# Moving the loads and splits of the first two head pairs around the bias stage of an attention kernel

## The chip, the cores and the metric

The kernel runs on one core of a Trainium2 chip. The metric is the device time of one execution in microseconds. Three runs of the kernel before took 463.45, 464.14 and 468.85; the median, 464.14, is what the change is compared with. All other times here are microseconds from the start of the span of one profiled execution.

## The reference

Attention with a learned relative-position bias, then two mixture-of-experts stages. The change touches the first part alone:

```python
scores = scale * np.matmul(q, k.transpose(0, 1, 3, 2))
rel = (pos[:, None] - pos[None, :]).astype(np.float32)
psi_rel = np.log1p(np.abs(rel))
psi_i = np.log1p(np.maximum(pos[:, None].astype(np.float32), 1.0))
x = (psi_rel / psi_i)[..., None]
h = np.maximum(x @ w1 + b1, 0.0)          # 32 hidden units
bias = h @ w2                             # 8 heads
scores = scores + bias.transpose(2, 0, 1)[None, :, :, :]
...                                       # softmax over the last axis
return np.matmul(attn, v).astype(np.float32)
```

q, k and v are 4 x 8 x 576 x 64 (batch, heads, sequence, head size). The bias is the same for all four batches; w1, b1 and w2 are inputs, so it has to be computed.

## The kernel before

**Constants.** Small tables and the weights of the bias network come first, some in SyncE's queue (`sel`, `pib`, `ident`, `phi_sb`, `w10`, part of `wsm`), some in ScalarE's (`ll`, the log table of 576 KB; the rest of `wsm`; `ipi`). A first matmul of `sel` and `wsm` spreads the weights over the partitions. VectorE copies them (`wrp`, `w2b`), scales the tables `pib`, `nib` and `ll` by them, and rounds `ident` to `identr`.

**Bias stage.** 36 batches `bt`, in the order 16..23, 0..15, 32..35, 24..31. One batch makes four hidden tiles `hid` of 128 x 576 (L215 on VectorE, L217 on ScalarE for one tile of three batches in four; 12 buffers), multiplies them with `w2b` on TensorE (L219), evicts the result on ScalarE to `ev` (L222; 6 buffers), and stores `ev` through SyncE to `scratch` in DRAM (L224). After batches 23, 7, 15, 35 and 31 SyncE loads the finished bias rows of the first head pair back from `scratch` (L285; L288 to L290 for the short last tile `biasm`). SyncE issues in program order, so what stands behind such a load waits with it.

**Attention.** 16 units, called pairs here: a pair of heads of one batch. For each, `tq`, `tk` and `tn` are loaded (`LQ`, `LK`, `LV`; one buffer each for `tq` and `tk`), and GpSimd splits q and k into a rounded high part (L383: `QHI`, `KHI`) and a low part (L385: `QLO`, `KLO`) in `sq` and `sk`, one buffer each. TensorE transposes these (L416, L444), ScalarE evicts them to `k` and `qT`, and the score matmuls follow (L461). VectorE adds the bias (L478), ScalarE takes the exponential (L485), GpSimd makes a high fp16 part of it (L496, `HI`), VectorE the low part (L500, `LO`), and SyncE transposes both by DMA. GpSimd also makes the low part of v (L404, `VLO`) and a swapped copy of k (L433, `SW`).

**What sets the order.** A table `SCHED` gives each step of a pair a due time. The steps before the first score matmul, and for the second pair `LK`, `LQ`, `KHI`, `KLO`, `QHI`, `QLO` (the function `x_early`), are written out before the bias stage (`early`); all others follow it in the order of their due times. In the bias stage only SyncE's queue is fixed to the written order. The other engines are ordered there by a scheduler from a model of the timeline; behind the bias stage all engines keep the written order.

Of the kernel before, what the change touches and what calls it, by code (L numbers as in the profile page):

```python
# [9 lines left out]
F32 = mybir.dt.float32  # L10
# [4 lines left out]
ALU = mybir.AluOpType  # L15
# [5 lines left out]
P = 128  # L21
NU = 9
HID = 32
# [89 lines left out]
def soft_moe_attention_kernel(ctx, tc, q, k, v, w1, b1, w2, phi, mw1, mw2,  # L113
                              skip, gate, gw1, gw2, c_ll, c_pi, c_ipi, c_sel, c_id, c_rk, out):
    nc = tc.nc
    sync, act, vec, pool, pe = nc.sync, nc.scalar, nc.vector, nc.gpsimd, nc.tensor
# [5 lines left out]
    ident = const.tile([P, P], F32, name="ident")  # L122
    sel = const.tile([P, P], F32, name="sel")
    phi_sb = const.tile([P, 4, NSL], F32, name="phi_sb")
# [3 lines left out]
    identr = const.tile([P, P], F32R, name="identr")  # L128
# [8 lines left out]
    w10 = const.tile([P, 4, 10], F32, name="w10")  # L137
# [19 lines left out]
    ps_t = actx.enter_context(tc.tile_pool(name="ps_t", bufs=2, space=PSUM))  # L157
# [5 lines left out]
    with ExitStack():  # L163
# [3 lines left out]
        ll = bc.tile([P, LLW], F32, name="ll")  # L167
        pib = bc.tile([P, 144], F32, name="pib")
        nib = bc.tile([P, 144], F32, name="nib")
        ipi = bc.tile([P, 36], F32, name="ipi")  # L170
        wsm = bc.tile([HID, 10], F32, name="wsm")
        wrp = bc.tile([P, 10], F32, name="wrp")
        w2b = bc.tile([P, 32], F32, name="w2b")
        offs = [bc.tile([P, 1], F32, name=f"offs{i}") for i in range(2)]
        vec.memset(w2b, 0.0)
        vec.memset(offs[0], 0.0)
        sync.dma_start(out=sel, in_=c_sel)
        act.dma_start(out=wsm[:, 0:1], in_=w1.rearrange("o m -> m o"))
        sync.dma_start(out=wsm[:, 2:10], in_=w2)
        act.dma_start(out=wsm[:, 1:2], in_=b1.rearrange("(m o) -> m o", o=1))  # L180
        sync.dma_start(out=pib, in_=c_pi)
        act.dma_start(out=ll, in_=c_ll)
        act.dma_start(out=ipi, in_=c_ipi)
        sync.dma_start(out=ident, in_=c_id)
        sync.dma_start(out=phi_sb, in_=phi.rearrange("(k p) s -> p k s", p=P))
        sync.dma_start(out=w10[:, :, 0:8], in_=gate.rearrange("(k p) e -> p k e", p=P))
        sync.dma_start(out=w10[:, :, 8:9], in_=skip.rearrange("(k p o) -> p k o", p=P, o=1))
        pw = ps_t.tile([P, 512], F32, name="pt")
        pe.matmul(pw[:, 0:10], lhsT=sel[0:HID, :], rhs=wsm, start=True, stop=True)
        vec.tensor_copy(wrp, pw[:, 0:10])  # L190
        for g in range(4):
            vec.tensor_copy(w2b[g * 32:(g + 1) * 32, g * 8:(g + 1) * 8], wrp[g * 32:(g + 1) * 32, 2:10])
        vec.tensor_scalar(out=pib, in0=pib, scalar1=wrp[:, 1:2], scalar2=None, op0=ALU.mult)
        vec.tensor_scalar(out=nib, in0=pib, scalar1=-1.0, scalar2=None, op0=ALU.mult)
        vec.tensor_scalar(out=ll, in0=ll, scalar1=wrp[:, 0:1], scalar2=None, op0=ALU.mult)
        vec.tensor_copy(identr, ident)

        po = ps_t.tile([P, 512], F32, name="pt")
        for c in range(4):
            pe.matmul(po[c * 32:(c + 1) * 32, 0:1], lhsT=w2b, rhs=wrp[:, 1:2], start=True, stop=True)  # L200
        vec.tensor_scalar(out=offs[1], in0=po[:, 0:1], scalar1=-1.0, scalar2=None, op0=ALU.mult)
        vec.tensor_copy(offs[0][0:96], offs[1][0:96])

        def bias_batch(bt):
            r, m4 = bt // 4, bt % 4
# [583 lines left out]
    OPS = [ops_of(n) for n in range(NP)]  # L789
# [6 lines left out]
    def x_early(x):  # L796
        return x in ("LK", "LQ", "KHI", "KLO", "QHI", "QLO")

    todo = sorted((n * II + place(n, x), n, x) for n in range(NP) for x in OPS[n])
    first = min(SC[x] for x in SC if x[:2] == "QK")  # L800
    early = [y for y in todo if y[0] < first or y[1] == 1 and x_early(y[2])]
    for t_, n, x in early:
        if (n, x) != (0, "SW"):
            OPS[n][x]()
    todo = [y for y in todo if y not in early]

# [2 lines left out]
    with tc.manual_schedule(engines={mybir.EngineType.SP}):  # L809
        for bt in order:  # L810
            bias_batch(bt)
            if bt % 8 == 7 or bt == 35:
                load_bias(0, bt // 8)
            if bt == 3:
                OPS[0]["SW"]()
    bctx.close()
    wctx = ExitStack()
    xpool = ctx.enter_context(tc.tile_pool(name="xpool", bufs=1, side="right"))
# [6 lines left out]
    with tc.manual_schedule(engines=fixed):  # L825
        last_td = max(place(NP - 1, f"TD{t}") for t in range(3)) + (NP - 1) * II
        lead_after = last_bias[0].ins
        lead = next(y for y in todo if y[2][0] == "L" and y[2][1] in "KQV" or y[2][:2] == "TD")
        for y in todo:
            t_, n, x = y  # L830
            with tc.issue_after(lead_after) if y == lead else ExitStack():
                OPS[n][x]()
            if t_ == last_td:
                while len(wq) < NW + 10:
                    weight_piece()
# [24 lines left out]
    SW = const.tile([P, 10], F32R, name="SW")  # L860
# [17 lines left out]
    held, sis = [], sl[1]  # L878
# [9 lines left out]
    with ExitStack() as mctx:  # L888
# [38 lines left out]
        for i in range(32):  # L927
            e, r = i // 4, i % 4
            o = e * P + r * NSL
            for j in range(4):  # L930
                pe.matmul(ph[j * 32:(j + 1) * 32, :], lhsT=sT[:, o:o + NSL],
                          rhs=wq[i][:, j * 256:(j + 1) * 256], start=(i == 0), stop=(i == 31))
# [6 lines left out]
        pt = ps.tile([P, 512], F32, name="pc")  # L939
# [550 lines left out]
```

## Time and profile before

| what | value |
|---|---|
| median of three runs | 464.14 |
| profiled execution | 465.27 |
| its span | 463.4 |
| busy: TensorE, VectorE, ScalarE, GpSimd | 416.3, 356.1, 309.5, 277.4 |
| mean granted TensorE clock | 0.985 |
| HBM read, written | 63.82 MB, 15.34 MB |

The span is what lies between the first and the last instruction; the execution takes 1.9 more. The busy sums cover stages with different limits. The bias stage takes up the first 64 us or so, the 16 pairs about the next 250, and the rest is weight loading and the two expert stages. For this change the views by time are of use: the timeline of one engine over the first 90 us, what ended each of its idle times, and when transfers landed.

### The profile page before, as it was taken

How to read it: one execution, taken by the hardware profiler on the slowest of the kernel's cores; microseconds unless marked ns; L12 is line 12 of the kernel's file. 1: busy time of each engine (PE TensorE's matmuls, PEld its weight loads, DVE VectorE, ACT ScalarE, POOL GpSimd, SP SyncE). 2: the span in 40 equal slices, each digit the busy share in tenths (PEclk: the TensorE clock that was granted, in tenths of full speed). 3: DMA queues.
4: the chain of work that ended last, by engine and by line, in shares of the span. 5: the costliest groups of instructions: out<-in, count | busy, mean ns of one | idle time of the engine just before them, and what ended most of it. 6: DMA issues, size and time to landing. Idle time of an engine off the chain costs nothing.

```text
span 463.4 us, 11519 instructions
## 1 busy us (share of the span) xinstructions
PE 416.3 (90%) x4314; PEld 303.8 (66%) x4314; DVE 356.1 (77%) x824; ACT 309.5 (67%) x650; POOL 277.4 (60%) x241
## 2 busy tenths in 40 slices
PE   3989997999999999999999999988899688899993
PEld 2545466887988888888888888786545221246572
DVE  5999977989889988988999978989645800118883
ACT  3997869798998998898889888697321300028710
POOL 4599508999999999999999989856120000001100
PEclk9999998999999999999999999999999889999998
DMA  6578768799988988998999997969999999992076
GB/s 179 197 240 269 269 231 212 199 168 217 247 204 170 247 197 171 228 233 185 190 230 241 167 218 135 191 127 198 302 412 407 404 410 409 409 343 102 24 204 214
DMA packets 145883, 108.92 MB, mean 235 GB/s; under 512 B 117952, under 2 KB 120512, under 8 KB 145824
## 3 DMA queue, kind: packets, MB, share of 16 engines
q1 hardware_dynamic: 143920, 104.91, 83.3%
q10 hardware_dynamic: 1824, 2.97, 2.0%
q8 instruction: 36, 0.59, 0.5%
q0 software_dynamic: 80, 0.26, 0.2%
q14 instruction: 23, 0.19, 0.1%
HBM read 63.82 MB, written 15.34 MB: 171 GB/s over the span
## 4 chain that ended last, share of the span: by engine, by line
PE 35%; DMA 21%; DVE 20%; POOL 8%; issue 7%; ACT 6%; ACTq 0%; SPq 0%; DVEq 0%; POOLq 0%
DVE ehl L500 9%; PE sc L461 7%; DMA x<-in_moe_w_dram 7%; DMA k<-in_moe_w_dram 6%; DVE e L478 5%; PE sc L219 5%; ACT ev L222 2%; PE pt L553 2%; DMA w2e<-in_moe_w_dram 2%; DMA tn<-in_v_dram 2%; PE av L590 2%; DMA bias<-in_moe_w_dram 2%; POOL k L433 1%; PE pt L696 1%; DVE em L478 1%
## 5 line engine op out<-in xcount | busy, mean ns | idle before, releaser
L485 ACT ACTIVATE e<-e,st 128x576 f32<-128x576 f32 x128 | 97.6, 776 | 16.1 <-DVE st L478 15.2
L478 DVE CUSTOM_DVE_ANT_0 e<-sc,bias 128x576 f32<-128x576 f32 x128 | 94.6, 749 | 13.0 <-PE sc L461 12.2
L461 PE MATMUL sc<-k,qT 128*128 128x288 f32 x512 | 96.9, 317 | 8.3 <-DVE st L478 6.0
L500 DVE SCALAR_TENSOR_TENSOR ehl<-e,ehl 128x1152 f16<-128x1152 f32 x48 | 88.7, 1867 | 0.9 <-POOL ehl L496 0.7
L461 PEld LDWEIGHTS sc<-k,qT 128*128 128x128 f32 x512 | 72.8, 191 | 18.8 <-DVE st L478 6.7
L496 POOL TENSOR_SCALAR ehl<-e 128x1152 f16<-128x1152 f32 x48 | 57.9, 1214 | 10.6 <-ACT e L485 8.9
L433 POOL TENSOR_SCALAR k<-k 64x1152 fp32r<-64x1152 f32 x30 | 59.8, 1995 | 3.0 <-ACT k L449 0.7
L219 PE MATMUL sc<-hid,w2b 128*32 128x288 f32 x576 | 52.7, 426 | 6.4 <-DVE hid L215 3.2
L215 DVE TENSOR_SCALAR hid<-ll,nib 128x576 f32<-128x576 f32 x117 | 56.7, 568 | 0.0
L590 PE MATMUL av<-v,eT 128*128 128x65 f16 x1152 | 50.0, 194 | 0.0
L219 PEld LDWEIGHTS sc<-hid,w2b 128*32 128x32 f32 x576 | 27.2, 112 | 29.7 <-ACT ev L222 12.9
L590 PEld LDWEIGHTS <-eT 128*128 128x128 f16 x1152 | 44.1, 98 | 0.6
L383 POOL TENSOR_SCALAR sk<-tk 128x576 fp32r<-128x576 f32 x16 | 39.7, 2484 | 5.4 <-PE pt L444 5.3
L1161 POOL TENSOR_SCALAR Lt<-rk 128x128 f16<-128x128 f32 x1 | 0.3, 297 | 66.6 <-PE pbig L1047 66.6
L222 ACT ACTIVATE ev<-sc,offs,ipi 128x576 f32<-128x576 f32 x36 | 30.0, 834 | 8.8 <-PE sc L219 6.8
L404 POOL TENSOR_TENSOR v<-tv,v 128x650 f16<-128x650 f32 x16 | 22.9, 1432 | 17.8 <-ACT v L400 17.8
L598 PE MATMUL av<-eq,tv 128*64 128x192 f32 x320 | 29.5, 331 | 0.0
L553 PE MATMUL pt<-ident,e 128*128 128x128 f32 x144 | 24.5, 282 | 4.5 <-DVE xnat L660 2.4
L1008 DVE COPY part<-pbig 128x256 f32<-128x256 f32 x2 | 0.9, 426 | 34.5 <-ACT part L1007 34.5
L1007 ACT COPY part<-pbig 128x256 f32<-128x256 f32 x2 | 0.7, 372 | 37.5 <-PE pbig L1047 37.5
L385 POOL TENSOR_TENSOR sq<-tq,sq 128x576 fp32r<-128x576 f32 x16 | 24.2, 1515 | 0.3
L598 PEld LDWEIGHTS av<-eq,tv 128*64 128x64 f32 x320 | 21.6, 137 | 4.2 <-issue 1.0
(338 smaller groups left out, 890.6 us busy)
## 6 DMA issues: line engine op xcount, KB each, us to landing
scratch<-ev SPq DMA_DIRECT2D x36, 288.0 KB, 4.7
bias<-scratch SPq DMA_DIRECT2D x16, 576.0 KB, 4.7
x<-in_moe_w_dram SPq DMA_DIRECT2D x18, 512.0 KB, 10.2
k<-in_moe_w_dram SPq DMA_DIRECT2D x14, 512.0 KB, 10.2
bias<-in_moe_w_dram SPq DMA_DIRECT2D x13, 512.0 KB, 9.3
tq<-in_q_dram SPq DMA_DIRECT2D x16, 288.0 KB, 3.8
tk<-in_k_dram SPq DMA_DIRECT2D x16, 288.0 KB, 4.7
tn<-in_v_dram SPq DMA_DIRECT2D x16, 288.0 KB, 4.9
```

Source lines behind the costliest of these rows:

```text
L215: vec.tensor_scalar(out=hid, in0=src, scalar1=nib[:, gi:gi + 1], scalar2=None, op0=ALU.max)
L219: pe.matmul(pb[c * 32:(c + 1) * 32, hh, 0:288], lhsT=w2b, rhs=hid[:, hh * 288:(hh + 1) * 288], start=True, stop=True)
L222: act.activation(ev, pb[:, :, 0:288].rearrange("p a (l u) -> p u a l", u=NU), AF.Identity, bias=offs[not on_act], scale=ipi[:, bt:bt + 1])
L383: pool.tensor_scalar(out=sx[:, :, 0, :], in0=t, scalar1=1.0, scalar2=1.0, op0=ALU.mult, op1=ALU.mult)
L433: pool.tensor_scalar(out=k1[64 * i:64 * i + 64], in0=k0[64 - 64 * i:128 - 64 * i], scalar1=1.0, scalar2=1.0, op0=ALU.mult, op1=ALU.mult)
L461: pe.matmul(sc[:, hh, 0:288], lhsT=l_, rhs=kf[i][:, o:o + 288], start=(i == 0), stop=(i == 1))
L478: vec.tensor_tensor_reduce(out=z["e", t][:, o].rearrange("p (a j) -> p a j", a=2), in0=z.pop(("sc", t, j))[:, :, 0:288], in1=bias_t[hp, t] ...
L485: act.activation(ee, ee, AF.Exp, bias=z["m", t][:, j:j + 1], scale=-1.0, **kw)
L496: pool.tensor_scalar(out=eh[:, 0], in0=z["e", t], scalar1=ES, scalar2=1.0, op0=ALU.mult, op1=ALU.mult)
L500: vec.scalar_tensor_tensor(out=eh[:, 1], in0=z.pop(("e", t)), scalar=ES, in1=eh[:, 0], op0=ALU.mult, op1=ALU.subtract)
L590: pe.matmul(av[:, oj:oj + VD], lhsT=eT[:, ei, 5 * j + c], rhs=v16[:, vi, 6 * j + c], start=False, stop=lastt and k_ == 2 and c == 3)
L598: pe.matmul(z["av", 1][j * 64:(j + 1) * 64, o], lhsT=tv[:, 6 * j + c if c < 4 else 4 + j, 0:64], rhs=z["eq"][:, 4 * j + c if c < 4 else 8] ...
```

## The change

The constants, their loads and the first matmuls become a function `prepare()`, which is called after the steps of all pairs have been defined. In it `LQ` of the first pair is the first load in SyncE's queue and `LK` the fifth; the log table is the first in ScalarE's. The six early steps of the second pair leave the place ahead of the bias stage: `LK` and `LQ` are written behind the store of batch 26, the third of the last eight, and `KHI`, `KLO`, `QHI`, `QLO` behind the whole stage, ahead of all its other steps. No instruction is added or taken away.

```diff
-        act.dma_start(out=wsm[:, 0:1], in_=w1.rearrange("o m -> m o"))
...
-        act.dma_start(out=ll, in_=c_ll)
...
+        def prepare():
+            vec.memset(w2b, 0.0)
+            vec.memset(offs[0], 0.0)
+            OPS[0]["LQ"]()
+            act.dma_start(out=ll, in_=c_ll)
+            sync.dma_start(out=sel, in_=c_sel)
+            act.dma_start(out=wsm[:, 0:1], in_=w1.rearrange("o m -> m o"))
+            act.dma_start(out=wsm[:, 1:2], in_=b1.rearrange("(m o) -> m o", o=1))
+            sync.dma_start(out=wsm[:, 2:10], in_=w2)
+            act.dma_start(out=ipi, in_=c_ipi)
+            sync.dma_start(out=pib, in_=c_pi)
+            OPS[0]["LK"]()
+            sync.dma_start(out=ident, in_=c_id)
...
     early = [y for y in todo if y[0] < first or y[1] == 1 and x_early(y[2])]
+    prepare()
+    held = [y for y in early if y[1] == 1 and x_early(y[2])]
     for t_, n, x in early:
-        if (n, x) != (0, "SW"):
+        if (n, x) not in ((0, "SW"), (0, "LQ"), (0, "LK")) and (t_, n, x) not in held:
             OPS[n][x]()
...
             if bt == 3:
                 OPS[0]["SW"]()
+            if bt == 26:
+                OPS[1]["LK"]()
+                OPS[1]["LQ"]()
...
         lead_after = last_bias[0].ins
+        for x in ("KHI", "KLO", "QHI", "QLO"):
+            OPS[1][x]()
```

SyncE's queue at the start of the program, before (the second `tq` is that of the second pair; its `tk` follows behind the store that stands last here; line numbers are those of each kernel):

```order
L177 DMA sel<-in_c_sel_dram 128x128
L179 DMA wsm<-in_w_dram 32x8
L181 DMA pib<-in_c_pi_dram 128x144
L184 DMA ident<-in_c_id_dram 128x128
L185 DMA phi_sb<-in_moe_phi_dram 128x4x32
L186 DMA w_73<-in_moe_w_gate_dram 128x4x8
L187 DMA w_73<-in_moe_w_skip_dram 128x4x1
L354 DMA tq<-in_q_dram 128x576
L349 DMA tk<-in_k_dram 128x576
L359 DMA tn<-in_v_dram 128x576 x2
L354 DMA tq<-in_q_dram 128x576
L224 DMA scratch<-ev 128x576
```

and now:

```order
L357 DMA tq<-in_q_dram 128x576
L180 DMA sel<-in_c_sel_dram 128x128
L183 DMA wsm<-in_w_dram 32x8
L185 DMA pib<-in_c_pi_dram 128x144
L352 DMA tk<-in_k_dram 128x576
L187 DMA ident<-in_c_id_dram 128x128
L188 DMA phi_sb<-in_moe_phi_dram 128x4x32
L189 DMA w_73<-in_moe_w_gate_dram 128x4x8
L190 DMA w_73<-in_moe_w_skip_dram 128x4x1
L362 DMA tn<-in_v_dram 128x576 x2
L227 DMA scratch<-ev 128x576 x8
```

The first pair's `tq` went from eighth to first place and its `tk` from ninth to fifth, ahead of `ident`; the second pair's two loads are gone from between the first stores. In ScalarE's queue the order `w1`, `b1`, `ll`, `ipi` became `ll`, `w1`, `b1`, `ipi`.

SyncE's queue at the end of the bias stage, before:

```order
L224 DMA scratch<-ev 128x576 x4
L288 DMA biasm<-scratch 64x576
L289 DMA biasm<-scratch 64x512
L290 DMA biasm<-scratch 64x64
L224 DMA scratch<-ev 128x576 x8
L285 DMA bias_973<-scratch 128x1152
L354 DMA tq<-in_q_dram 128x576
L349 DMA tk<-in_k_dram 128x576
```

and now:

```order
L227 DMA scratch<-ev 128x576 x4
L291 DMA biasm<-scratch 64x576
L292 DMA biasm<-scratch 64x512
L293 DMA biasm<-scratch 64x64
L227 DMA scratch<-ev 128x576 x3
L352 DMA tk<-in_k_dram 128x576
L357 DMA tq<-in_q_dram 128x576
L227 DMA scratch<-ev 128x576 x5
L288 DMA bias_967<-scratch 128x1152
L357 DMA tq<-in_q_dram 128x576
```

The second pair's `tk` and `tq` stand between the third and the fourth of the last eight stores; five stores and the last bias load stand behind them.

GpSimd's split instructions and what follows them, before (the first four are the first pair's, the next four the second pair's):

```order
L383 TENSOR_SCALAR sq<-tq 128x9x64
L385 TENSOR_TENSOR sq<-tq,sq 128x9x64
L383 TENSOR_SCALAR sk<-tk 128x9x64
L385 TENSOR_TENSOR sk<-tk,sk 128x9x64
L383 TENSOR_SCALAR sk<-tk 128x9x64
L385 TENSOR_TENSOR sk<-tk,sk 128x9x64
L383 TENSOR_SCALAR sq<-tq 128x9x64
L385 TENSOR_TENSOR sq<-tq,sq 128x9x64
L404 TENSOR_TENSOR v_1021<-tv_170,v_1021 128x650
L496 TENSOR_SCALAR ehl<-e 128x1152 x2
```

and now:

```order
L386 TENSOR_SCALAR sq<-tq 128x9x64
L275 MEMSET tv_140 64x65 x2
L388 TENSOR_TENSOR sq<-tq,sq 128x9x64
L386 TENSOR_SCALAR sk<-tk 128x9x64
L388 TENSOR_TENSOR sk<-tk,sk 128x9x64
L386 TENSOR_SCALAR sk<-tk 128x9x64
L388 TENSOR_TENSOR sk<-tk,sk 128x9x64
L386 TENSOR_SCALAR sq<-tq 128x9x64
L388 TENSOR_TENSOR sq<-tq,sq 128x9x64
L407 TENSOR_TENSOR v_1021<-tv_139,v_1021 128x650
L499 TENSOR_SCALAR ehl<-e 128x1152 x2
```

The order of the two splits stays the same. What moved is the place of the second pair's in the program: its inputs now come at the end of the bias stage, and the low part of v and the first `ehl` high parts still stand behind it.

## Rows read from the trace of the kernel before

**Rows 1.** Timeline of SyncE's queue, 24 to 75: start, duration, instruction

```profile
27.16 0.32 SPq L285 DMA_DIRECT2D bias<-scratch  x1
...
40.44 0.32 SPq L285 DMA_DIRECT2D bias<-scratch  x1
...
50.84 0.32 SPq L285 DMA_DIRECT2D bias<-scratch  x1
...
58.85 0.48 SPq L288 DMA_DIRECT2D biasm<-scratch  x1
...
60.72 7.04 SPq L224 DMA_DIRECT2D scratch<-ev  x8
...
70.28 0.32 SPq L285 DMA_DIRECT2D bias<-scratch  x1
```

**Rows 2.** Waits of SyncE's queue, 24 to 72: sum, times, longest

```profile
SPq L285 <- DMA scratch<-ev: 10.3, 4, 4.2
```

**Rows 3.** DMA issues, 0 to 4: KB each, us from issue to landing

```profile
ll<-in_c_ll_dram ACTq DMA_DIRECT2D x1, 576.0 KB, 4.7
...
wsm<-in_b_dram ACTq DMA_DIRECT2D x1, 0.1 KB, 1.9
```

**Rows 4.** DMA issues of the stores at 60.72, then at 62.24

```profile
scratch<-ev SPq DMA_DIRECT2D x1, 288.0 KB, 2.3
...
scratch<-ev SPq DMA_DIRECT2D x1, 288.0 KB, 5.0
```

**Rows 5.** Timeline of ScalarE; in brackets the idle time before

```profile
7.23 2.11 ACT L217 ACTIVATE hid<-ll,pib 128x576 f32<-128x576 f32 x3 [3.31 <-DVE ll L195]
...
10.80 0.47 ACT L395 ACTIVATE tv<-tn 64x320 f32<-64x320 f32 x1 [1.46 <-DMA tn<-in_v_dram]
...
15.68 0.83 ACT L222 ACTIVATE ev<-sc,offs,ipi 128x576 f32<-128x576 f32 x1 [0.73 <-PE sc L219]
...
24.16 0.89 ACT L222 ACTIVATE ev<-sc,offs,ipi 128x576 f32<-128x576 f32 x1
...
45.65 0.83 ACT L222 ACTIVATE ev<-sc,offs,ipi 128x576 f32<-128x576 f32 x1 [1.84 <-DMA scratch<-ev]
...
63.52 0.83 ACT L222 ACTIVATE ev<-sc,offs,ipi 128x576 f32<-128x576 f32 x1 [0.51 <-PE sc L219]
```

**Rows 6.** Two stretches, hidden tiles (L215) alone: VectorE busy (instructions), clock, DMA

```profile
20.00:46.00 26.00, 26.00 (x61) 1.00 0.74 248
47.80:52.60 4.80, 4.80 (x5) 1.00 0.62 181
```

**Rows 7.** Timeline of VectorE, 0 to 64

```profile
3.86 0.17 DVE L190 COPY wrp<-pt 128x10 f32<-128x10 f32 x1 [2.95 <-PE pt L189]
...
5.64 0.30 DVE L193 TENSOR_SCALAR pib<-pib,wrp 128x144 f32<-128x144 f32 x1 [0.89 <-DMA pib<-in_c_pi_dram]
...
7.24 56.67 DVE L215 TENSOR_SCALAR hid<-ll,nib 128x576 f32<-128x576 f32 x117
```

**Rows 8.** Timeline of GpSimd, 7 to 92

```profile
8.73 0.85 POOL L383 TENSOR_SCALAR sq<-tq 128x576 fp32r<-128x576 f32 x1 [5.30 <-DMA tq<-in_q_dram]
...
18.96 29.44 POOL L383 TENSOR_SCALAR sk<-tk 128x576 fp32r<-128x576 f32 x1 [5.34 <-PE pt L444]
...
68.77 1.43 POOL L404 TENSOR_TENSOR v<-tv,v 128x650 f16<-128x650 f32 x1 [16.35 <-ACT v L400]
...
71.11 2.27 POOL L496 TENSOR_SCALAR ehl<-e 128x1152 f16<-128x1152 f32 x2 [0.90 <-ACT e L485]
...
79.64 0.67 POOL L383 TENSOR_SCALAR sk<-tk 128x576 fp32r<-128x576 f32 x1
...
81.32 1.44 POOL L385 TENSOR_TENSOR sk<-tk,sk 128x576 fp32r<-128x576 f32 x1
...
82.71 2.55 POOL L385 TENSOR_TENSOR sq<-tq,sq 128x576 fp32r<-128x576 f32 x1
```

**Rows 9.** One stretch: each engine busy (instructions), clock, DMA share, GB/s

```profile
62.00:67.00 5.00, 5.00 (x42) 2.80 (x36) 2.67 (x7) 2.08 (x3) 0.00 (x0) 1.00 1.02 384
```

More of the change, by code (lines that the diff above doesn't have):

```diff
@@ L174, in soft_moe_attention_kernel @@
         offs = [bc.tile([P, 1], F32, name=f"offs{i}") for i in range(2)]
-        vec.memset(w2b, 0.0)
-        vec.memset(offs[0], 0.0)
-        sync.dma_start(out=sel, in_=c_sel)
-        act.dma_start(out=wsm[:, 0:1], in_=w1.rearrange("o m -> m o"))
-        sync.dma_start(out=wsm[:, 2:10], in_=w2)
-        act.dma_start(out=wsm[:, 1:2], in_=b1.rearrange("(m o) -> m o", o=1))
-        sync.dma_start(out=pib, in_=c_pi)
-        act.dma_start(out=ll, in_=c_ll)
-        act.dma_start(out=ipi, in_=c_ipi)
@@ L184, in soft_moe_attention_kernel @@
[L184 to L201, printed above, removed]
@@ L202, in soft_moe_attention_kernel @@
-        vec.tensor_copy(offs[0][0:96], offs[1][0:96])
+        def prepare():
[11 more added lines that the diff above has]
+            sync.dma_start(out=ident, in_=c_id)
+            sync.dma_start(out=phi_sb, in_=phi.rearrange("(k p) s -> p k s", p=P))
+            sync.dma_start(out=w10[:, :, 0:8], in_=gate.rearrange("(k p) e -> p k e", p=P))
+            sync.dma_start(out=w10[:, :, 8:9], in_=skip.rearrange("(k p o) -> p k o", p=P, o=1))
+            pw = ps_t.tile([P, 512], F32, name="pt")
+            pe.matmul(pw[:, 0:10], lhsT=sel[0:HID, :], rhs=wsm, start=True, stop=True)
+            vec.tensor_copy(wrp, pw[:, 0:10])
+            for g in range(4):
+                vec.tensor_copy(w2b[g * 32:(g + 1) * 32, g * 8:(g + 1) * 8], wrp[g * 32:(g + 1) * 32, 2:10])
+            vec.tensor_scalar(out=pib, in0=pib, scalar1=wrp[:, 1:2], scalar2=None, op0=ALU.mult)
+            vec.tensor_scalar(out=nib, in0=pib, scalar1=-1.0, scalar2=None, op0=ALU.mult)
+            vec.tensor_scalar(out=ll, in0=ll, scalar1=wrp[:, 0:1], scalar2=None, op0=ALU.mult)
+            vec.tensor_copy(identr, ident)
+            po = ps_t.tile([P, 512], F32, name="pt")
+            for c in range(4):
+                pe.matmul(po[c * 32:(c + 1) * 32, 0:1], lhsT=w2b, rhs=wrp[:, 1:2], start=True, stop=True)
+            vec.tensor_scalar(out=offs[1], in0=po[:, 0:1], scalar1=-1.0, scalar2=None, op0=ALU.mult)
+            vec.tensor_copy(offs[0][0:96], offs[1][0:96])
```

## The prediction

> **What bounds the kernel now.** The change touches the first 75 us alone, so I read that stretch: first the queue of SyncE, then ScalarE, VectorE and GpSimd.
>
> SyncE. Each of the 36 bias batches ends in an eviction on ScalarE and a store of it to the DRAM scratch. After batches 8, 16, 24, 28 and 36 of the order SyncE loads finished bias rows back, and issues nothing behind that load until the stores before it have landed. The loads go out at 27.16, 40.44, 50.84, 58.85 and 70.28 [rows 1], four of them after 10.3 us of waiting for landings [rows 2]. With an empty queue a transfer lands in about 2 us, like the small constant of [rows 3]; the store issued at 62.24 took 5.0 [rows 4]. So from 27.16 on the stage runs as a serial chain: load, the stores behind it, wait, load. What starts the chain is the eighth eviction, which ends at 24.16 + 0.89 = 25.05 [rows 5].
>
> ScalarE. At 45.65 an eviction waits 1.84 us for a store to land, since there are six eviction buffers [rows 5]: the chain holds the compute, not the other way round. ScalarE comes loose from it only near the end, where the eviction at 63.52 waits for TensorE.
>
> VectorE. 61 hidden tiles, the first and last cut, fall in 26 us: one per 0.43 us [rows 6]. All 117 would take 50.3, they took 56.67 [rows 7]: 6.4 us are lost. In 47.8 to 52.6 only five were touched [rows 6], beside GpSimd's instructions [rows 8]. GpSimd does two splits of a pair in the stage, so one costs VectorE 3.2 us. The other side of this: the first instruction of the second pair's split stands for 29.44 us, from 18.96 to 48.40 [rows 8].
>
> GpSimd. From 71.11 on it has nearly no idle time: ten instructions stand back to back before the one at 82.71 [rows 8]. What comes late there is late for good; I take a shift of its 71.11 to pass unchanged to the end.
>
> **The change part by part.**
>
> *The start.* The log table and q now stand ahead of the small constants in their own queues. The first matmul needs four of those; the last to come is b1, issued at 1.21 and 1.9 us on the way, so in at 3.1. VectorE's first copy is at 3.86, its hidden tiles start at 7.24, with 0.89 of waiting for the pi table in between [rows 7]. Low bound: the constants come only one issue later, 0.45, and the pi wait goes: 7.24 + 0.45 - 0.89, 0.4 early. High bound: they land with the log table, 4.7 us after its issue [rows 3] at 0.74, so at 5.4: 2.3 later, less 0.9, hidden tiles at 8.6, 1.4 late. I take the high bound: the table of [rows 3] is 576 KB and needs most of its 4.7 us for data, and b1 is behind it. The Trainium skill, DMA: Bandwidth & Descriptors, Queues, rings and completion order, says that a DMA engine takes the descriptors of one ring in order and changes between rings at packets; by that the term is +1.4, without it -0.4. No row of before has a small transfer behind a big one in ScalarE's queue to show it.
>
> *The first pair's split.* Its q is in by about 5.5, where GpSimd now waits for it until 8.73 [rows 8], so two of its four instructions run while VectorE still waits for constants. Half of 3.2 stays on the hidden tiles: 1.6 saved against 1.4 lost. ScalarE decides: it makes three hidden tiles (2.11 us, from 7.23) once the table is scaled, waits for v until 10.80, and is then busy to 25.05, but for one wait of 0.73 on TensorE [rows 5]. The table is scaled by 8.1, half a microsecond ahead of the hidden tiles, or by 9.3, if q's split, which runs from 5.5 to some 7.5, holds up the small copies ahead of it. So ScalarE is through with its three tiles between 10.2 and 11.4, and the wait of 0.73, behind hidden tiles that GpSimd delayed, may go. The chain starts between 1.3 us earlier and 0.6 later; I take 0.5 earlier.
>
> *The second pair's split leaves the stage.* VectorE gets 3.2 us back. None of it shortens the chain: with the hidden tiles earlier, the evictions wait for buffers. The 35th, now at 63.52, needs the store issued at 60.72 landed, which takes 2.3 more [rows 4]: 63.0. So 0.5 is saved at the tail beside the 0.5 of the start, and the first scores, behind that eviction, come 1.0 earlier. If the chain were loose all 3.2 would show: that is the other end.
>
> *The two loads in the new place.* They go out behind the third of the last eight stores, at about 62.2. At 384 GB/s [rows 9] a 288 KB transfer takes 0.77. The first of the eight is in at 63.0, so three are in at 64.5, k at 65.3, q at 66.1. GpSimd is idle there: its next work is at 68.77 [rows 8]. The four instructions take 0.67 + 1.44 + 0.67 + 1.44 plus gaps of 0.1, so they end at 69.8 and v's low part, 1.43, at 71.2. Today GpSimd starts the high parts at 71.11, after 0.9 of idle time [rows 8]. Less the 0.5 of the start this is 70.7: **0.4 us earlier**, since GpSimd's queue gives less than the 1.0 its inputs gain. Ends: 0 and 1.0 of gain if k comes as computed, up to 2.0 of loss if not (below). Five stores come 1.5 us later, and the last bias load goes out at about 71.3 and, at the 4.7 of the table of the same size in [rows 3], lands at 76.0; its tile is first added behind two low parts on VectorE that wait for GpSimd, so this costs nothing, unless those come earlier by as much.
>
> *Taken out of the early part:* two loads at 11 to 14 us, which nothing waited behind.
>
> Sum: -0.4. The profiled execution took 465.27, which is 1.1 above the median of the three runs, 464.14. So 464.9 for a profiled run, and **463.7** for the median.
>
> **The rivals.**
>
> *VectorE is the path.* For it: its hidden tiles never pause [rows 7], and TensorE and ScalarE follow them. Then 3.2 plus the 0.5 of the start come through: 460.4. Against it: the 1.84 at 45.65, and the landings. It needs k early as well, or GpSimd takes back what is won. 0.2.
>
> *Slower: k comes late and GpSimd's queue is the path.* The store issued at 62.24 was in at 67.2 [rows 4], 1.9 later than its place in the queue asks for. Now k's load stands in just that place. With the 0.5 of the start k is in at 66.7 instead of 64.8; the split ends at 71.2, v's low part at 72.6, and the high parts start 1.5 later than now: 465.6. From a k that lands after 65.2 on, GpSimd loses. If the last instruction of the split reaches VectorE's low parts it is stretched as at 82.71, where one took 2.55 [rows 8] instead of 1.44: 1.1 more, and with nothing won at the start another 0.5: 467.2. The Trainium skill, SBUF — State Buffer, Who interferes with whom, gives a reason: a VectorE instruction with two SBUF inputs shuts out one of GpSimd that reads SBUF; the 2.55 agrees. The order of after shows the split ahead of v's low part and the high parts on GpSimd, so this price has no cover. 0.25.
>
> *Slower: the start.* If k of the first pair meets the hidden tiles as 18.96 did, GpSimd waits until VectorE's twelve buffers are full, 12 x 0.43 = 5.2 us, while TensorE stands at k's transposes. The chain starts some 1.5 late: 465.6. Against it: at 8.73 GpSimd got in at once [rows 8]. 0.1.
>
> **How the numbers follow.** The forecast, the chain with GpSimd's queue just in time, has 0.45, and 463.7; the rivals 0.2, 0.25 and 0.1. All of them lie within 2% (9.3 us), about what a measurement of this kernel can tell from no change. The range runs from the first rival to the late k with its stretch: 460.4 to 467.2. Over 2% either way nothing in these rows reaches; I leave 0.02 and 0.03 for a shift that meets the later transfers in another way: 0.02 faster, 0.95 same, 0.03 slower.
>
> **What would show it.** Right: hidden tiles start near 8.6 and run without a long one in mid-stage; the first bias load goes out near 26.7, the later ones at the old distances; evictions wait for landings more than now; GpSimd's second split begins near 65 and its first high part near 70.7. The first bias load at 27.7 or later shows the start as wrong. Later bias loads closer together show the chain as wrong, and the first rival right. A split that ends after 71 shows the second. The sum is wrong wholly if GpSimd's shift at 71 is not the shift of the end.

## The result and the profile after

The change made the kernel slower: 470.15 us against 466.26 (medians of 20 runs each), a ratio of 1.0087 with a 95% interval of 1.0069 to 1.0105. The profiled execution took 470.14, its span 468.3; that of before 465.27 and 463.4. So the two profiles differ by 4.9, the medians by 3.9. The ratios here and below leave out executions over 1.5% above the fastest of their kernel.

SyncE's queue in the changed kernel, for [rows 1] (start, duration, instruction; line numbers are 3 higher):

```profile
29.42 0.32 SPq L288 DMA_DIRECT2D bias<-scratch  x1
42.50 0.32 SPq L288 DMA_DIRECT2D bias<-scratch  x1
53.08 0.32 SPq L288 DMA_DIRECT2D bias<-scratch  x1
61.47 0.48 SPq L291 DMA_DIRECT2D biasm<-scratch  x1
...
63.61 2.81 SPq L227 DMA_DIRECT2D scratch<-ev  x3
66.46 0.46 SPq L352 DMA_DIRECT2D tk<-in_k_dram  x1
...
74.88 0.32 SPq L288 DMA_DIRECT2D bias<-scratch  x1
```

The first four loads are 2.26, 2.06, 2.24 and 2.62 late, the last 4.6. The chain kept its distances, and VectorE's freed time did not shorten it. The 2 us of the start come from here, VectorE's timeline, for [rows 7] (the line of `ll` is the scaling of the log table, which ScalarE's first tiles wait for):

```profile
7.26 0.17 DVE L193 COPY wrp<-pt 128x10 f32<-128x10 f32 x1 [6.36 <-PE pt L192]
7.47 1.75 DVE L195 COPY w2b<-wrp 32x8 f32<-32x8 f32 x4
9.25 1.37 DVE L196 TENSOR_SCALAR pib<-pib,wrp 128x144 f32<-128x144 f32 x1
10.54 0.81 DVE L198 TENSOR_SCALAR ll<-ll,wrp 128x1152 f32<-128x1152 f32 x1
...
11.61 0.51 DVE L218 TENSOR_SCALAR hid<-ll,nib 128x576 f32<-128x576 f32 x1
...
69.09 0.76 DVE L481 CUSTOM_DVE_ANT_0 e<-sc,bias 128x576 f32<-128x576 f32 x1 [5.35 <-PE sc L464]
```

The first copy is 3.4 late, and then the small operations are slow: `pib` took 0.30 in before [rows 7], and `w2b` 0.69, in the first line here; the second is the scaling of the log table, also of before.

```profile
4.06 0.69 DVE L192 COPY w2b<-wrp 32x8 f32<-32x8 f32 x4
...
6.38 0.81 DVE L195 TENSOR_SCALAR ll<-ll,wrp 128x1152 f32<-128x1152 f32 x1
```

The scaling is 4.2 late, and the hidden tiles start 4.4 late. The DMA issues of 0 to 4 (KB each, us to landing), for [rows 3], and GpSimd's timeline, for [rows 8]:

```profile
ll<-in_c_ll_dram ACTq DMA_DIRECT2D x1, 576.0 KB, 4.7
tq<-in_q_dram SPq DMA_DIRECT2D x1, 288.0 KB, 4.9
...
wsm<-in_b_dram ACTq DMA_DIRECT2D x1, 0.1 KB, 4.6
wsm<-in_w_dram SPq DMA_DIRECT2D x1, 1.0 KB, 4.7
```

```profile
5.82 0.67 POOL L386 TENSOR_SCALAR sq<-tq 128x576 fp32r<-128x576 f32 x1 [2.77 <-DMA tq<-in_q_dram]
...
6.87 1.39 POOL L388 TENSOR_TENSOR sq<-tq,sq 128x576 fp32r<-128x576 f32 x1
8.34 0.67 POOL L386 TENSOR_SCALAR sk<-tk 128x576 fp32r<-128x576 f32 x1
9.10 1.43 POOL L388 TENSOR_TENSOR sk<-tk,sk 128x576 fp32r<-128x576 f32 x1
70.58 0.67 POOL L386 TENSOR_SCALAR sk<-tk 128x576 fp32r<-128x576 f32 x1 [60.05 <-DMA tk<-in_k_dram]
...
74.90 1.43 POOL L407 TENSOR_TENSOR v<-tv,v 128x650 f16<-128x650 f32 x1
76.30 2.25 POOL L499 TENSOR_SCALAR ehl<-e 128x1152 f16<-128x1152 f32 x2
```

A constant of 0.1 KB behind the log table lands 4.6 us after its issue, where [rows 3] had 1.9. GpSimd's first split stands from 5.82 to 10.53 beside exactly those small operations of VectorE. At the end of the stage the second pair's k lands at 70.4 (3.9 after its issue), GpSimd has no idle time from there, and its first high part starts 5.2 later than in before. The loss so grows from 2.3 at the chain to 5.2; the span ends 4.9 later. ScalarE, for [rows 5]: the 35th eviction waits for a buffer, that is for the first of the last eight stores, issued at 63.61; in before it had a wait for TensorE of 0.51 there.

```profile
67.38 0.83 ACT L225 ACTIVATE ev<-sc,offs,ipi 128x576 f32<-128x576 f32 x1 [3.64 <-DMA scratch<-ev]
```

### The profile page after: what moved, and what is told of

Read it like the earlier page. It is cut to its first block, busy times and chain, and to the rows that moved or that the text cites. A ratio compares the mean times of both kernels' runs of the same rounds, so it can differ in the third digit from the quotient of the medians.

```text
span 468.3 us, 11523 instructions
## 1 busy us (share of the span) xinstructions
PE 411.8 (88%) x4314; PEld 300.4 (64%) x4314; DVE 352.9 (75%) x824; ACT 308.9 (66%) x650; POOL 247.9 (53%) x241
## 4 chain that ended last, share of the span: by engine, by line
PE 31%; DMA 22%; DVE 21%; POOL 10%; issue 7%; ACT 6%; SPq 1%; DVEq 0%; POOLq 0%; ACTq 0%
DVE ehl L503 10%; DMA x<-in_moe_w_dram 7%; DMA k<-in_moe_w_dram 6%; PE sc L464 6%; DVE e L481 4%; ACT ev L225 3%; PE sc L222 3%; PE pt L556 3%; DMA scratch<-ev 2%; DMA w2e<-in_moe_w_dram 2%; PE av L593 2%; DMA bias<-in_moe_w_dram 2%; POOL ehl L499 2%; POOL sq L388 2%; POOL sk L388 1%
## 5 line engine op out<-in xcount | busy, mean ns | idle before, releaser
L222 PE MATMUL sc<-hid,w2b 128*32 128x288 f32 x576 | 45.7, 433 | 9.3 <-ACT ev L225 6.5
L218 DVE TENSOR_SCALAR hid<-ll,nib 128x576 f32<-128x576 f32 x117 | 50.9, 514 | 1.3 <-PE sc L222 1.1
L386 POOL TENSOR_SCALAR sk<-tk 128x576 fp32r<-128x576 f32 x16 | 10.7, 672 | 60.2 <-DMA tk<-in_k_dram 60.0
L222 PEld LDWEIGHTS sc<-hid,w2b 128*32 128x32 f32 x576 | 20.4, 113 | 31.9 <-ACT ev L225 20.5
L220 ACT ACTIVATE hid<-ll,pib 128x576 f32<-128x576 f32 x27 | 20.7, 774 | 7.5 <-DVE ll L198 7.5
L388 POOL TENSOR_TENSOR sk<-tk,sk 128x576 fp32r<-128x576 f32 x16 | 24.1, 1504 | 0.3
```

Source lines behind the costliest of these rows:

```text
L218: vec.tensor_scalar(out=hid, in0=src, scalar1=nib[:, gi:gi + 1], scalar2=None, op0=ALU.max)
L222: pe.matmul(pb[c * 32:(c + 1) * 32, hh, 0:288], lhsT=w2b, rhs=hid[:, hh * 288:(hh + 1) * 288], start=True, stop=True)
```

## The experiments

My theory after these rows: the start costs about 2 at the chain, since constants land behind large transfers and the early split holds up VectorE's small operations; the rest is lost at the tail, where the chain holds the 35th eviction and k comes late. The rivals: the start is absorbed, or VectorE bounds the stage. Fourteen kernels were run. In the table are the places that decide, each from the timelines of one profiled execution, and the ratio of the runs to those of before on the same chip. Before had a median of 466.55 beside start_alone, table_first, pair_alone and pair_in_gap, 465.91 beside q_first, late_m, late_all and late_all_pair, 467.02 beside start_held, gap8, eight_ev and after_late, and 467.04 beside pair8 and after8. A profile can lie off its median: that of start_alone is of an execution of 467.63, 2.9 below, that of q_first of one of 470.15, 1.7 above. table_first stands in its own paragraph.

| kernel | hidden tiles start | 1st bias load | 35th eviction | 1st score add | 1st high part | span | median | ratio, 95% interval |
|---|---|---|---|---|---|---|---|---|
| before | 7.24 | 27.16 | 63.52 | 65.44 | 71.11 | 463.4 | | |
| after | 11.61 | 29.42 | 67.38 | 69.09 | 76.30 | 468.3 | 470.15 | 1.0087 (1.0069 to 1.0105) |
| start_alone | 12.12 | 30.89 | 66.15 | 67.86 | 73.65 | 465.8 | 470.52 | 1.0075 (1.0045 to 1.0105) |
| start_held | 10.03 | 29.19 | 65.91 | 67.84 | 73.51 | 465.5 | 467.74 | 1.0040 (1.0007 to 1.0073) |
| q_first | 10.17 | 28.84 | 67.19 | 68.90 | 75.60 | 468.3 | 468.50 | 1.0049 (1.0015 to 1.0083) |
| pair_alone | 7.02 | 26.66 | 64.14 | 66.39 | 73.56 | 464.9 | 468.34 | 1.0025 (0.9998 to 1.0052) |
| pair_in_gap | 6.95 | 27.00 | 63.91 | 66.16 | 73.33 | 464.9 | 467.55 | 1.0018 (0.9992 to 1.0045) |
| pair8 | 7.18 | 27.22 | 60.24 | 62.22 | 72.76 | 465.1 | 469.46 | 1.0039 (1.0002 to 1.0075) |
| gap8 | 7.34 | 27.39 | 60.40 | 62.38 | 68.00 | 461.6 | 463.41 | 0.9922 (0.9889 to 0.9954) |
| late_m | 7.22 | 27.28 | 61.53 | 63.25 | 68.91 | 460.8 | 463.71 | 0.9948 (0.9923 to 0.9972) |
| late_all | 7.24 | 29.23 | 60.36 | 62.29 | 67.96 | 459.5 | 462.33 | 0.9921 (0.9893 to 0.9949) |
| late_all_pair | 7.11 | 29.09 | 60.22 | 62.15 | 67.82 | 459.0 | 461.98 | 0.9919 (0.9888 to 0.9950) |
| eight_ev | 7.15 | 27.05 | 60.20 | 62.17 | 67.79 | 460.0 | 463.34 | 0.9927 (0.9894 to 0.9960) |
| after_late | 11.96 | 32.36 | 62.96 | 64.88 | 70.55 | 461.9 | 463.74 | 0.9948 (0.9918 to 0.9978) |
| after8 | 12.18 | 30.13 | 62.61 | 64.59 | 75.27 | 469.6 | 471.15 | 1.0088 (1.0058 to 1.0118) |

**The start, four kernels.** start_alone is the changed kernel without its second part:

```diff
-    held = [y for y in early if y[1] == 1 and x_early(y[2])]
+    held = []
...
-            if bt == 26:
-                OPS[1]["LK"]()
-                OPS[1]["LQ"]()
...
-        for x in ("KHI", "KLO", "QHI", "QLO"):
-            OPS[1][x]()
```

> Only the new start; the second pair's loads and split stay ahead of the bias stage as before. Theory (constants land behind the big transfers, and the first pair's split then runs against VectorE's small operations): wrp at about 7.3, hidden tiles from about 11.6, first bias load at about 29.4 (27.16 before), first high part at about 73 (71.1 before), total about 2 us above before. Rival A (the start is absorbed, the whole loss comes from the second pair's late k): first bias load within 0.5 of 27.2, total within 0.5 of before. Rival B (the start costs all 4.5): first high part at 75.5 or later.

Measured: the first high part (73.65) is near the theory's 73, and rival A is out. The first bias load, at 30.89, is 1.5 later than forecast: GpSimd's second split, which in before stood until 48, here got in at once and slowed the hidden tiles until 24.67, ahead of that load.

```profile
19.23 0.98 POOL L386 TENSOR_SCALAR sk<-tk 128x576 fp32r<-128x576 f32 x1 [8.19 <-PE pt L447]
```

By the ratio the total is 3.5 above before, 1.5 more than forecast.

table_first moves the log table to the front of ScalarE's queue in before, and nothing else.

> Only the log table goes to the front of ScalarE's queue; the first pair's q and k stay behind the constants in SyncE's queue, the second pair as before. Theory: w1 and b1 land behind the table at about 5.5 to 6.2 instead of 3.1, wrp at about 6.5; the first pair's q comes at about 8.7 as before, so GpSimd does not hold up VectorE's small operations (w2b copies 0.16 each, pib 0.30); hidden tiles from about 9.3; first bias load at about 28.5, total about 1 us above before. If lateness of the constants were the whole loss of the start, first bias load at 29.4; if the split's collision were, 27.2.

Measured: ratio 1.0005 (0.9974 to 1.0036), where about 1 us was expected. The profiled execution took 475.73, some 9 above the median of its runs, 467.13, so only its first microseconds are read here. VectorE:

```profile
7.35 0.29 DVE L194 TENSOR_SCALAR pib<-pib,wrp 128x144 f32<-128x144 f32 x1
...
8.56 0.52 DVE L216 TENSOR_SCALAR hid<-ll,nib 128x576 f32<-128x576 f32 x1
```

and GpSimd:

```profile
10.57 5.54 POOL L384 TENSOR_SCALAR sq<-tq 128x576 fp32r<-128x576 f32 x1 [7.14 <-DMA tq<-in_q_dram]
```

Late constants alone give hidden tiles at 8.56 in this one execution, just the 8.6 of the forecast; by the ratio they cost 0.2 at the end, with an interval from 1.2 below to 1.7 above. This execution then shows a collision like that of the third rival, with q's split in the place of k's: it met the hidden tiles and stood for 5.54, and the first bias load went out at 33.85.

q_first is start_alone with `ll` back behind `w1` and `b1`.

> As the run with the new start alone, but the log table goes back behind w1 and b1 in ScalarE's queue; the first pair's q stays first and k fifth in SyncE's. Theory (what costs at the start is mostly the early split of q and k that holds up VectorE's small operations, and any large transfer ahead of the constants): wrp at about 5 (the constants of SyncE's queue land behind q), one of w2b's copies or pib at 0.6 us or more beside GpSimd's split, hidden tiles from 9 to 10.5, first bias load at 28.3 to 29.4, total 1.5 to 3 above before. Rival (the log table ahead of w1 and b1 is the whole loss of the start): wrp at 4.2 or earlier, hidden tiles from at most 7.8, total within 0.7 of before.

Measured: `wrp` at 5.14, `pib` takes 1.43 beside the split, hidden tiles at 10.17, median 2.6 above before (2.3 by the ratio). So q at the front costs, with or without the table.

start_held is start_alone with the split of q held until the pi table is scaled:

```diff
+                if x == "q" and not held_split:
+                    held_split.append(1)
+                    pool.tensor_scalar(out=sx[:, 0, 0, 0:16], in0=nib[:, 0:16], scalar1=1.0, scalar2=1.0, op0=ALU.mult, op1=ALU.mult)
```

> As the run with the new start alone, with one small GpSimd instruction ahead of the first pair's split that reads the scaled pi table, so that the split cannot run beside VectorE's small operations. Theory (split and small operations get in each other's way, 2 us at the start): w2b's four copies at 0.7 us together instead of 1.8, pib at 0.3 instead of 1.5, hidden tiles at 9.5 to 10 instead of 12.1; the split then meets the hidden tiles and costs them up to 3.2 us as in before, or stands beside them as at 18.96 there: first bias load at 28 to 29.5 if it gets in, total 1 to 2.5 above before; later than 30 if it stands. Rival (the small operations are slow for another reason): pib still over 1 us, hidden tiles at 11.5 or later.

Measured on VectorE:

```profile
7.55 0.69 DVE L195 COPY w2b<-wrp 32x8 f32<-32x8 f32 x4
8.28 0.29 DVE L196 TENSOR_SCALAR pib<-pib,wrp 128x144 f32<-128x144 f32 x1
```

The same operations at the same place take their old time, and the hidden tiles start 2.1 earlier than in start_alone. So the collision of split and small operations is real. What it costs at the chain is not shown: the first bias load goes out 1.7 earlier than in start_alone, but there the second split got in ahead of it, while here it stood until 50.75. The changed kernel has the collision and no second split there, and its load, at 29.42, is only 0.2 behind start_held, where the first split slows hidden tiles instead. The ratio falls from 1.0075 to 1.0040, with intervals that overlap. Over the four kernels the totals go with the start of the hidden tiles: 1.3 late in table_first, 2.8 in start_held, 2.9 in q_first and 4.9 in start_alone, against 0.2, 1.9, 2.3 and 3.5 by the ratios.

**The second pair alone.** pair_alone is before with `held`, the loads behind batch 26 and the split behind the stage; pair_in_gap has the two loads at batch 35 instead, ahead of the short bias tile.

> Only the second pair's part: start as before, its loads behind the third of the last eight stores, its split behind the bias stage. Theory (the stage is bound by the chain of loads, stores and landings; late k then makes GpSimd's queue the path): bias loads at 27.2, 40.4, 50.8, 58.9 within 0.5 though VectorE gets 3.2 us back; k lands at about 68, first high part about 2 to 2.5 us later than before (73.1 to 73.6), total about 2.4 above before. Rival (VectorE bounds the stage): bias loads closer together, the fourth 2 us or more earlier than 58.9. The recorded forecast's account: k in by 65.3, first high part at about 71, total within 0.5 of before.

> As the run with the second pair's part alone, but k and q are loaded ahead of the short last bias tile, in the stretch from 58.4 to 60.1 where SyncE and the DMA queues stand still. Theory (the late k is what costs, not the split's place behind the stage): k in at about 60, split at 60 to 66 against few remaining hidden tiles, first high part at 70.5 to 71.3, total between 0.7 below and 0.3 above before. Rival (the split behind the stage costs by itself, whenever k comes): first high part at 72.5 or later, total 1.5 or more above.

Measured: in pair_in_gap the first four bias loads stand within 0.5 of before, as the chain theory has it, though the hidden tiles end at 60.5 instead of 63.9. In pair_alone they come 0.5, 0.9, 0.8 and 1.4 earlier, three of them outside the 0.5 allowed, but short of the 2 of the rival; k landed at 66.1 there, where 68 was expected. VectorE's 3.2 us shorten nothing at the end. k in the gap, landed by 58.9, gave a first high part at 73.33 against 73.56, so late k did not decide here; that expectation failed. The rival's high part came true, its total did not: the ratios stand for 1.2 and 0.8 above before, and both intervals include no change. TensorE of pair_in_gap, and the stretches 64 to 70 (each engine busy, clock, DMA share, GB/s):

```profile
64.79 1.33 PE L461 MATMUL sc<-k,qT 128*128 128x288 f32 x4 [3.15 <-ACT ev L222]
66.05 2.13 PE L219 MATMUL sc<-hid,w2b 128*32 128x288 f32 x4
68.11 3.19 PE L461 MATMUL sc<-k,qT 128*128 128x288 f32 x12
```

```profile
64.00:66.00 2.00, 1.21 (x4) 0.98 (x4) 0.00 (x0) 0.74 (x1) 0.64 (x1) 0.50 1.02 392
66.00:68.00 2.00, 2.00 (x5) 0.54 (x4) 0.77 (x2) 0.00 (x0) 0.00 (x0) 0.50 0.80 304
68.00:70.00 2.00, 2.00 (x8) 1.83 (x8) 0.53 (x1) 1.73 (x3) 0.00 (x0) 0.50 0.02 9
```

TensorE, done early, stands for the 35th eviction, and its clock is 0.50, the lower level, until after 70. In before the same four matmuls take 0.79 and 1.16:

```profile
64.62 0.79 PE L461 MATMUL sc<-k,qT 128*128 128x288 f32 x4
65.33 1.16 PE L219 MATMUL sc<-hid,w2b 128*32 128x288 f32 x4
```

The 35th eviction itself is late since the store that it waits for lands 3.6 after its issue, where [rows 4] had 2.3. In that time one packet of instructions passes. DMA of pair_in_gap, 60.8 to 61.2 (queue: packets, MB, share of 16 engines):

```profile
q8 instruction: 1, 0.02, 18.5%
```

and of before, 65.0 to 65.5:

```profile
q8 instruction: 1, 0.02, 11.5%
```

The share times 16 engines times the window gives 1.2 and 0.9 us on one DMA engine. In before it comes after that store has landed. In the eleven profiles with these loads in their old places (table_first apart) it comes within 1.4 us of VectorE's last hidden tile, so ending the tiles earlier seems to pull it forward. The store took 2.3 in the three where the packet came later (before, start_alone, start_held), and 3.2 to 4.4 in the eight where it fell on the store. That the packet delays the store is read from this agreement; no run moved it by itself, and its own 0.9 to 1.5 us do not explain the whole delay (2.1 in pair_alone, with a packet of 0.9). The Trainium skill, Runtime: NRT & Kernel Launch, Instruction fetch mechanics, says that engines fetch their code in 16 KB blocks at a cost that is mostly hidden: the size of the packet agrees, and if it is the cause, its cost here is 0.9 to 2.1 us of one store.

**The chain taken away.** late_m is pair_in_gap with the short bias tile loaded behind the sixth of the last eight stores; in late_all (from before) and late_all_pair every load stands three stores later:

```diff
-            if bt % 8 == 7 or bt == 35:
-                load_bias(0, bt // 8)
+            k3 = order.index(bt) - 3
+            if k3 >= 0 and (order[k3] % 8 == 7 or order[k3] == 35):
+                load_bias(0, order[k3] // 8)
+            if bt == 31:
+                load_bias(0, 3)
```

> As the run that loads k and q in the gap, but the short last bias tile is loaded behind the sixth of the last eight stores instead of ahead of the first. Theory (the chain holds the tail: the last eight stores wait behind that load, the 35th eviction waits 3.7 us for a buffer, TensorE stands still and its clock falls to half until 71): without it the eviction does not wait, the clock stays at 1.00 from 60 to 70, the first score add on VectorE comes at 62 to 63.5 instead of 66.2, first high part at 68 to 70 instead of 73.3, total 1.5 to 3 below before. Rival (what is late is something else, as the last rows of bias or GpSimd): first high part within 1 of 73.3 and total within 0.7 of the run in the gap.

> Before, with every load of finished bias rows written three stores later than its last store (the fourth full one as before, behind the last store): SyncE waits less, and the stores are not held. The second pair's split stays in the stage. Chain theory: no eviction waits over 0.5 us for a landing; VectorE still loses 3.2 us to that split and ends its hidden tiles at 62 to 64 as before; so VectorE becomes the bound and the total is 0 to 1 below before. Rival (the chain alone bounds, compute has 3 us in hand): hidden tiles end at 61 or earlier and the total is 2 or more below before.

> The same late loads, with the second pair's loads written behind the store of the 28th batch and its split behind the stage, so both the chain and VectorE's 3.2 us are taken away. Chain theory: the gains now add up: hidden tiles end at 60.5 or earlier, first score add at 61.5 to 63, clock at 1.00 through 60 to 70, first high part at 67.5 to 69.5, total 2 to 3.5 below before. Rival (the 3.2 us of VectorE are worth nothing even without the chain, ScalarE or TensorE bound the stage): first score add within 1 of the run with late loads alone, total within 1 of it.

Measured: late_m went as the theory has it, with the clock at 1.00 from 62 to 72 and 2.2 below before, but for a wait of 1.00 that the 35th eviction kept. late_all went by its rival: 3.6 below before, with the second split still in the stage, and without it (late_all_pair) no better. The reason is seen in eight_ev, which is before with one number changed:

```diff
-        ev_ = bctx.enter_context(tc.tile_pool(name="bev", bufs=6, side="right"))
+        ev_ = bctx.enter_context(tc.tile_pool(name="bev", bufs=8, side="right"))
```

> Before, with 8 instead of 6 buffers for the evicted bias; nothing else. Theory (the loads hold the stores, full buffers hold the evictions, VectorE then pauses near 48 and only in that pause does GpSimd's second split get in): the wait of 1.84 us at 45.65 goes, VectorE does not pause, the split stands until the hidden tiles end at about 60.7 instead of 63.9, first score add at 62.3 to 63.5 instead of 65.4, total 2 to 4 below before. Rival (VectorE's 3.2 us beside the split are lost in any case, buffers only move the wait): hidden tiles end at 63 or later, total within 0.7 of before.

Measured: its theory came true, with a ratio of 0.9927 (3.4 below before). VectorE, GpSimd and SyncE of eight_ev:

```profile
7.15 53.48 DVE L215 TENSOR_SCALAR hid<-ll,nib 128x576 f32<-128x576 f32 x117
```

```profile
18.84 42.32 POOL L383 TENSOR_SCALAR sk<-tk 128x576 fp32r<-128x576 f32 x1 [5.78 <-PE pt L444]
61.24 1.43 POOL L385 TENSOR_TENSOR sk<-tk,sk 128x576 fp32r<-128x576 f32 x1
```

```profile
58.60 0.48 SPq L288 DMA_DIRECT2D biasm<-scratch  x1
```

The bias loads stand within 0.3 of before up to this one (58.85 in [rows 1]): the chain did not move, it only holds the evictions no longer. The hidden tiles take 53.48 instead of the 56.67 of [rows 7]. The split's first instruction stands for 42.32, until the last hidden tile is done. In before it stood for 29.44 and got in near 48, after the eviction that had waited at 45.65 [rows 5]. How it can get in is seen in start_held, where the eviction at 48.48 had waited 2.3 for a landing. GpSimd, then VectorE:

```profile
18.41 32.34 POOL L389 TENSOR_SCALAR sk<-tk 128x576 fp32r<-128x576 f32 x1 [4.16 <-PE pt L450]
```

```profile
50.56 15.73 DVE L218 TENSOR_SCALAR hid<-ll,nib 128x576 f32<-128x576 f32 x30 [0.34 <-PE sc L222]
```

VectorE paused for 0.34 before 50.56, for a hidden buffer, and the split got in there. In before VectorE shows no pause near 48, and in start_alone none over 0.02 near 19.23, so how the split got in is open in these two. What eight_ev shows is that with two more buffers it does not get in, and VectorE does not lose the 3.2 us of the second split, which the change was to take off it; that full eviction buffers let the split in is inferred.

gap8 is pair_in_gap with 8 buffers; pair8 is pair_alone with 8; after8 and after_late are the changed kernel with 8 buffers and with the late loads (k and q behind batch 35).

> As the run that loads k and q in the gap (second pair's split behind the stage), with 8 buffers for the evicted bias. Theory (in the run with 6 a 16 KB fetch of instructions at 60.9 makes the first of the last eight stores land at 63.8 instead of 62.5, the 35th eviction waits for that buffer, TensorE stands and its clock falls): the fetch stays at about 61 and that store lands as late, but no eviction waits for it; the 35th eviction runs at about 60.8 instead of 63.9, clock 1.00 from 60 to 70, first high part at 67.8 to 69.5 instead of 73.3, total 2.5 to 4 below before. Rival (the late loads of bias rows at the end of the queue bound the first scores): first high part at 71 or later, total within 1 of before.

> The changed kernel with every load of finished bias rows three stores later and the second pair's k and q behind the store of the 28th batch, as in the run with late loads and the pair. Theory (the start's delay of VectorE and ScalarE is real work late, and without the chain nothing absorbs it): hidden tiles from 11.6 to about 63 (start 4.4 later, split's 3.2 us of the first pair not in them: 50.9 long), first score add at 63.5 to 65, total 1.5 to 2.5 above the run with late loads and the pair, and 1.5 to 3 below before. Rival (the start costs nothing once the chain is gone): total within 0.7 of the run with late loads and the pair.

> The second pair's part alone, k and q behind the third of the last eight stores as in the change, with 8 buffers for the evicted bias: as the run in the gap with 8 buffers, but for the place of the two loads. Theory (once no eviction waits, k's lateness is what is left of the change's second part): the 35th eviction at about 60.5, clock 1.00, k issued at about 62 and landed at 66 to 67.5, GpSimd back to back from there, first high part at 71.5 to 73 instead of 68.0, total 2.5 to 4.5 above the run in the gap with 8 buffers. Rival (k's place costs nothing, as between the two runs with 6 buffers, 73.56 and 73.33): first high part within 1 of 68.0, total within 1 of that run.

> The changed kernel with 8 buffers for the evicted bias and nothing else. Theory (the start, 2.1 at the chain, and the late k remain; the eviction's wait goes): the 35th eviction at about 64 to 65 instead of 67.4, k landed at 68 to 70.4, GpSimd back to back from there, first high part at 73.5 to 76, total 1 to 3.5 above before. Rival (the eviction's wait is the whole loss behind the start): first high part at 71 to 72, total below before.

Measured: in gap8 the first of the last eight stores lands as late as in pair_in_gap (3.5 after its issue), but nothing waits for it: 3.6 below before. pair8 differs from gap8 only in the place of k and q, and is 6.1 slower (5.5 by the ratios, 3.5 by the spans). TensorE and GpSimd of pair8:

```profile
69.30 0.75 PE L416 MATMUL pt<-identr,sk 128*128 128x128 f32 x4 [3.65 <-POOL sk L385]
69.84 1.29 PE L461 MATMUL sc<-k,qT 128*128 128x288 f32 x4
```

```profile
67.09 0.67 POOL L383 TENSOR_SCALAR sk<-tk 128x576 fp32r<-128x576 f32 x1 [53.12 <-DMA tk<-in_k_dram]
...
71.35 1.43 POOL L404 TENSOR_TENSOR v<-tv,v 128x650 f16<-128x650 f32 x1
72.76 2.25 POOL L496 TENSOR_SCALAR ehl<-e 128x1152 f16<-128x1152 f32 x2
```

k comes at 67; TensorE, whose written order has the second pair's transposes between the first pair's scores, stands 3.65 for its split, and GpSimd goes back to back to the first high part. TensorE's granted clock is 0.50 from 68 to 74, behind that standing time, where 1.00 was expected; in gap8, where it does not stand for the split, the clock is 1.00 until 74. So the late k cost TensorE its standing time and its clock too, and by the ratios it is beyond the 2.5 to 4.5 expected. With 6 buffers k's lateness was hidden behind the eviction, which is why pair_in_gap looked no better than pair_alone: there GpSimd still had 1.43 of idle time before its first high part. after8 is as slow as the changed kernel, 4.1 above before where 1 to 3.5 was expected, though no eviction waits: the late k takes over (landed at 69.4, first high part at 75.27). after_late stays above late_all_pair, by 2.9 in the spans and 1.4 by the ratios, whose intervals overlap: as far as it goes, that is the start, with the chain gone.

late_all_pair is the fastest of all by its median, but late_all, eight_ev and gap8 are within its interval; eight_ev needs the least edit.

## Why the prediction was wrong

The forecast of 463.7 (460.4 to 467.2) stood against a median of 464.14; the change cost 3.9 where -0.4 was forecast, and the new median lies above the range. Before itself had a median of 466.26 over 20 runs, 2.1 above that of the first three; even a range moved up by this ends at 469.3, below the measured 470.15.

- **What bounds the stage: right, for six buffers.** The distances of the first four bias loads held within 0.4, and 3.2 us on VectorE gave nothing there. eight_ev adds that this chain holds the compute only through the full buffers: with two more, the loads stand where they stood and 3.4 us are gained. That GpSimd's shift at 71 passes to the end held for the change: 5.2 there, 4.9 at the end. In the other kernels of the table the two differ by up to 2.0 (after8: 4.2 and 6.2).
- **The start term: wrong, the step that failed first.** "Hidden tiles at 8.6" and "the chain starts 0.5 earlier" became 11.61 and 2.1 later, outside the bounds of 1.3 earlier to 0.6 later. The term that was mis-sized is the scaling of the log table, which sets when ScalarE begins: done by 8.1 to 9.3 in the forecast, by 11.35 in the run. The constants behind the table were sized rightly by the high bound (8.56 in table_first). Two things were added: q, also in front, makes `wrp` later still (7.26 against 6.43), and the split's collision with VectorE's small operations, to which I gave 1.2 at most, took 2. I counted the early split as a gain of 1.6 because VectorE "still waits for constants" then. The late constants moved VectorE's small operations into that very stretch: `w2b` ran at 7.47 and `pib` at 9.25, amid the four instructions of the split. The gain itself was there, all 3.2 of it: no split slowed the hidden tiles any more, one per 0.43 from 12.11 on. But ScalarE, not VectorE, set the eighth eviction: it was busy from 11.38 until then but for one wait of 0.26.
- **ScalarE through with its three tiles by 11.4: wrong.** It began them at 11.38, 4.15 late, and ended at 13.5. The wait for v of [rows 5], 1.46, was covered by this, and the eighth eviction ended 2.1 late, at 27.17 instead of 25.05.
- **The 35th eviction: right wait, wrong size.** I let it wait for its store with the 2.3 us of [rows 4]. The store took 3.7 and was issued 2.9 later.
- **k in by 65.3: wrong, the step that failed at the tail.** It landed at 70.4, with the start as before (pair_alone) at 66.1. My second rival is what happened: k stands in the place of a store that had taken 5.0, and GpSimd's queue becomes the path. pair8 against gap8 shows the step. I priced it at up to 2.0, or 3.1 with a stretched instruction that did not come ahead of the first high part; between those two it is 3.5 (spans) to 5.5 (ratios), since TensorE waits as well and then runs at the lower clock.
- **Left out entirely:** TensorE's standing time. Work that ends early in front of a fixed wait leaves TensorE idle, and in pair_alone and pair_in_gap its clock fell to half just as the first scores came. In the changed kernel it stood too, but its clock was 1.00 there.
- **The first rival** (VectorE is the path) was wrong for the changed kernel, and the third (k of the first pair stands) did not occur in it; one execution of table_first showed its like, with q's split.

By the ratios the start alone costs 3.5 and the pair alone 1.2, against 4.1 together (3.9 by the medians). So most of the loss seems to be the start's; that the parts add up is within the intervals, and that of the pair alone includes no change.

## What to carry to other kernels

When a stage is a chain of transfers with waits, look at what makes it wait (buffers, a load written one store too early) before moving work off an engine beside it: two more buffers gave 3.4 us, and the moved work gave nothing. A load moved later is paid for at each engine whose written order has its consumer next, so follow it on all of them, and do not conclude from a run in which another wait covers it. Work moved to "while the other engine still waits" must be checked against where that wait itself moves.

## What the runs showed of the hardware that was not expected

- All eight transfers issued in the changed kernel's first 4 us landed 4.5 to 4.9 after their issue, from 0.1 to 576 KB.
- A GpSimd instruction of 0.67 us stood for 42.32 beside VectorE's unbroken row of 117 tiles, until the row ended. It need not be so: in start_alone the same instruction, at 19.23, took 0.98 beside such a row. The other way round, GpSimd's split slowed VectorE's `pib` from 0.30 to 1.37. The Trainium skill, SBUF — State Buffer, Who interferes with whom, lets the engine that issues first hold the ports that the two share for one whole instruction; that the loser can stand through a whole row of them, these traces show.
- TensorE's clock was 0.50 after 3.15 us of standing in pair_in_gap, but 1.00 after 3.09 in the changed kernel.
